# Attention and gated feed-forward on one core: the first third of the instructions of every engine in a listed order, the mask tables in fewer steps, tiles at other addresses

## The chip, the cores and the metric

The kernel runs on one core of a Trainium2 chip, as one launch. The metric is the device time of one execution in microseconds (us), as the median of several. A core has a matrix engine (TensorE, PE in the profile; its weight loads are a row of their own, PEld), a vector engine (VectorE, DVE), an activation engine (ScalarE, ACT), a general engine (GpSimd, POOL) and an engine that issues transfers (SyncE, SP). Each runs its own instructions strictly in the order in which they stand in the program, and semaphores make one engine wait for another. Of the memories, SBUF holds the tiles and PSUM takes what PE writes, in banks of 512 fp32 columns.

## The reference

Attention over 4 batches and 8 heads of 768 positions with 64 features each, with a local and a global mask and a bias that grows with distance; its output, 3,072 rows of 512, goes through a gated feed-forward of width 1,536.

```python
rel = pos[:, None] - pos[None, :]
is_global = pos[None, :] < int(n_global)                # n_global = 8
is_local = (rel >= 0) & (rel < int(n_local))            # n_local = 96
keep = is_global | is_local
dist = np.where(is_global & ~is_local, float(n_local), np.abs(rel))
scores = scale * q @ k.T - slopes * dist
scores = np.where(keep, scores, -1e9)
a = softmax(scores); x = a @ v
gate = 1 / (1 + np.exp(-(x @ w_gate)))
out = (gate * (x @ w_val)) @ w_out
```

The two counts and the three weights are handed over with 64 bits a number; the rest is fp32.

## The kernel before

**Work and tiling.** Rows are taken in 8 blocks of 3 x 128 (two blocks a batch). The attention of a block has four steps `s`, one for each pair of heads. A step has its scores (`scores`, L368 in the first two blocks, L382 later), a minimum with the bias table added (VectorE, L401), the exponential (ScalarE, L414), a transpose (TensorE with `ident`, L447, in the first two blocks; by DMA later), the product with `v` (`values`, L497) and, in the first block, row sums that are spread by a matmul (L523). Every query tile sees 256 keys at most: 96 previous ones, 32 global ones and its own 128. The feed-forward of a block runs over 12 slices `f` of the width: `ff_in` makes gate and value (24 matmuls of 384 columns a slice, L559, into `ps_g` and `ps_u`), `ff_out` adds the slice's part of the output (L599, into three banks `ps_o`).

**Precision by parts.** Most operands are split into a high and a low part (`xh`, `xl`; `w1h`, `w1l`; `w2h`, `w2l`; `hh`, `hl`) and each product is three matmuls. The weights arrive as 64-bit numbers and are turned to fp32 during the first block: `conv_a` and `conv_b` put the bits together on ScalarE and VectorE (L193, L200, L209), `conv_c` splits into `w1h` (ScalarE, L230) and `w1l` (GpSimd, L181, in 8 slices). The second weight is split again for each slice and block (`w2h` on ScalarE, L212; `w2l` on GpSimd, L181).

**Staging.** The attention of the first block stands alone at the start. After it, the attention of block `b + 1` is laid between the feed-forward slices of block `b`. The first block's slices meet their weights as these are converted.

**The start.** Two broadcasts bring the counts (`words`, L77, SyncE). Four VectorE instructions (L81 to L84) make floats of them, and `build_tables` (L107 to L145) makes the distance tables `dist` and `dist0` from counting patterns that GpSimd writes; `build_pair` (L158) scales them into the tables of each head. `keep_busy` (L97) gives TensorE matmuls on zeros, of which nothing is read.

**What sets the order.** The code is written in loops, and the framework's scheduler, which works with a simulated time, decides the order on each engine; `issue_after` holds single instructions behind others. Which addresses a tile has follows from the sizes of the pools that are opened before it.

Of the kernel before, what the change touches and what calls it, by code (L numbers as in the profile page):

```python
# [16 lines left out]
ALU = mybir.AluOpType  # L17
# [3 lines left out]
P = 128  # L21
PREV = 96
GLOB = 32
SLOT = GLOB + P
WIN = PREV + SLOT
NEG = 1.0e30


@with_exitstack
def attn_moe_kernel(ctx, tc, qT, kT, v, n_global, n_local, wg, wv, wo, out, B, H, S, D):  # L30
    nc = tc.nc
    DM = H * D
    NC = DM // P
# [23 lines left out]
    spool = inner.enter_context(tc.tile_pool(name="spool", bufs=2))  # L57
# [2 lines left out]
    wraw = cstack.enter_context(tc.tile_pool(name="wraw", bufs=1))  # L60
    late = {}

    def issue_after(later, earlier):
        tc.add_manual_dep(
            later.ins,
            earlier.ins.name,
            mybir.DependencyInfo(mybir.DependencyClass.NoSync, mybir.DependencyReason.DATA),
            reason="issue order",
        )


    nf = cpool.tile([P, 2], F32, name="nf")


    words = cpool.tile([P, 2, 2], I32, name="words")
    for k, src in enumerate((n_local, n_global)):
        nc.sync.dma_start(  # L77
            words[:, k], src.bitcast(I32)[0:2].rearrange("(a b) -> a b", a=1).to_broadcast([P, 2])
        )
    wf = cpool.tile([P, 3, 2], F32, name="wf")  # L80
    nc.vector.tensor_copy(wf[:, 0:2].rearrange("p w k -> p k w"), words)  # L81
    nc.vector.tensor_scalar(wf[:, 2], wf[:, 0], 0.0, None, op0=ALU.is_lt)
    nc.vector.tensor_tensor(wf[:, 2], wf[:, 2], wf[:, 1], op=ALU.add)
    nc.vector.scalar_tensor_tensor(nf, wf[:, 2], 2.0 ** 32, wf[:, 0], op0=ALU.mult, op1=ALU.add)  # L84
    ident = cpool.tile([P, P], F32, name="ident")
    warm = cpool.tile([P, 1], F32, name="warm")
    nc.vector.memset(warm, 0.0)
# [18 lines left out]
    tabs = [cpool.tile([P, WIN], BF16, name=f"tab{h}") for h in range(H)]  # L106
    tabs0 = [cpool.tile([P, P], BF16, name=f"tabs{h}") for h in range(H)]  # L107
    nms = cpool.tile([P, 2 * (B * NTB * NPAIR)], F32, name="nms")
    def build_tables():

        nl, ng = nf[:, 0:1], nf[:, 1:2]
        reli = spool.tile([P, WIN], I32, name="pT", tag="pT", bufs=PTB)
        nc.gpsimd.iota(reli[:, 0:PREV], pattern=[[-1, PREV]], base=PREV, channel_multiplier=1)
        nc.gpsimd.iota(reli[:, PREV:PREV + GLOB], pattern=[[1, GLOB]], base=0, channel_multiplier=0)
        nc.gpsimd.iota(reli[:, PREV + GLOB:WIN], pattern=[[-1, P]], base=0, channel_multiplier=1)
        coli = mpool.tile([P, P], I32, name="work", tag="work", bufs=WORKB)
        nc.gpsimd.iota(coli, pattern=[[1, P]], base=0, channel_multiplier=0)
        rel = spool.tile([P, WIN], F32, name="pT", tag="pT", bufs=PTB)
        nc.vector.tensor_copy(rel, reli)
        col = mpool.tile([P, 2, P], F32, name="work", tag="work", bufs=WORKB)  # L120
        nc.vector.tensor_copy(col[:, 0], coli)
        loc = spool.tile([P, WIN], F32, name="pT", tag="pT", bufs=PTB)
        pen = mpool.tile([P, 2, P], F32, name="work", tag="work", bufs=WORKB)
        cur = slice(PREV + GLOB, WIN)
        kg, only, both = col[:, 0], col[:, 1], pen[:, 0]
        nc.vector.tensor_scalar(loc, rel, 0.0, None, op0=ALU.is_ge)
        nc.vector.tensor_scalar(kg, kg, ng, None, op0=ALU.is_lt)
        nc.vector.scalar_tensor_tensor(loc, rel, nl, loc, op0=ALU.is_lt, op1=ALU.mult)
        nc.vector.tensor_tensor(rel, rel, loc, op=ALU.mult)
# [3 lines left out]
        nc.vector.tensor_tensor(only, kg, loc[:, cur], op=ALU.is_gt)  # L133
        nc.vector.tensor_tensor(both, kg, loc[:, cur], op=ALU.max)
        nc.vector.scalar_tensor_tensor(only, only, nl, rel[:, cur], op0=ALU.mult, op1=ALU.add)
        nc.vector.tensor_scalar(both, both, 1.0, NEG, op0=ALU.subtract, op1=ALU.mult)
        nc.vector.tensor_tensor(dist0, both, only, op=ALU.subtract)
        build_pair(0, True, (dist, dist0))

        gsl = slice(PREV, PREV + GLOB)  # L140
        nc.vector.tensor_copy(loc[:, gsl], kg[:, 0:GLOB])
        nc.vector.tensor_scalar(rel[:, gsl], kg[:, 0:GLOB], nl, None, op0=ALU.mult)
        nc.vector.tensor_scalar(loc, loc, 1.0, NEG, op0=ALU.subtract, op1=ALU.mult)
        nc.vector.tensor_tensor(dist, loc, rel, op=ALU.subtract)
        return dist, dist0  # L145

    built = set()
    last_min = []
# [3 lines left out]
    def build_pair(s, zero, dist):  # L152
        if (s, zero) in built:
            return
        built.add((s, zero))
        for h in (2 * s, 2 * s + 1):
            eng = nc.gpsimd if s else nc.vector
            eng.tensor_scalar((tabs0 if zero else tabs)[h], dist[zero], slopes[h] / SCALE, None, op0=ALU.mult)  # L158


    w1h = [wpool.tile([P, 2, NC, P], F32R, name=f"w1h{f}") for f in range(NF)]
# [192 lines left out]
    def scores(bi, s, t):  # L354
# [542 lines left out]
```

## Time and profile before

| what | value |
|---|---|
| time, median of 3 runs | 735.9 us (735.83 to 737.05) |
| profiled execution | 739.84 us, of which the instructions span 738.1 us |
| PE busy | 722.8 us, 98% of the span |
| weight loads, DVE, ACT, POOL busy | 655.9, 474.7, 410.8, 228.2 us |
| mean granted TensorE clock | 0.991 |

The profile is one execution, read by a hardware profiler. A busy share is an average over stages, and the ends of matmuls are modelled, so that PE is shown busy where a matmul is only stretched; the distance from one start to the next tells more. Idle time of an engine is printed with what ended it. Times on the line of an instruction are us from the start of the span.

### The profile page before, as it was taken

To read this page: it belongs to the slowest core of one execution; us is meant where nothing else is said; L and a number is where in the kernel's file an instruction comes from. 1 tells how busy PE (TensorE), PEld (TensorE's weight loads), DVE (VectorE), ACT (ScalarE), POOL (GpSimd) and SP (SyncE) were. 2 spreads that over 40 slices of the span, in tenths; PEclk is the share of its full clock that TensorE was granted. 3 is DMA by queue.
4 is the path that set the end of the run, shared out by engine and by line. 5 is a ranking of instruction groups with operands and counts; after the bars stand their busy time and mean duration, and the time that the engine had idled before them with its cause. 6 is when DMAs were issued, how large, how long until landed. Compare 5 with 4: busy or idle time off the path is not lost. (4 is left out here: it accounts for less than half of the span.)

```text
span 738.1 us, 12514 instructions
## 1 busy us (share of the span) xinstructions
PE 722.8 (98%) x4403; PEld 655.9 (89%) x4403; DVE 474.7 (64%) x1279; ACT 410.8 (56%) x938; POOL 228.2 (31%) x238
## 2 busy tenths in 40 slices
PE   8999999999999999999999999999999999999996
PEld 5758788989889999999999999999999999999995
DVE  6765577577877877776777777666787867321111
ACT  4787686656555555565456655555555664332222
POOL 5437366323222323232232323213232231221222
PEclk8999999999999999999999999999999999999999
DMA  8688573524455342442435442353435234010001
GB/s 256 182 256 273 175 211 101 134 56 88 101 89 152 83 110 68 91 113 58 87 84 112 118 102 69 52 133 75 96 78 112 72 44 86 16 44 1 1 0 46
DMA packets 136868, 74.28 MB, mean 101 GB/s; under 512 B 87136, under 2 KB 129120, under 8 KB 136800
## 3 DMA queue, kind: packets, MB, share of 16 engines
q1 hardware_dynamic: 136656, 73.17, 40.0%
q8 instruction: 36, 0.59, 0.4%
q14 instruction: 32, 0.26, 0.1%
q10 hardware_dynamic: 144, 0.26, 0.1%
HBM read 49.81 MB, written 6.29 MB: 76 GB/s over the span
## 5 line engine op out<-in xcount | busy, mean ns | idle before, releaser
L181 POOL TENSOR_TENSOR w2l<-w2f,w2h 128x512 fp32r<-128x512 f32 x89 | 120.3, 1351 | 361.9 <-ACT w2h L212 354.8
L559 PE MATMUL ps_g<-xh,w1l 128*128 128x384 f32 x384 | 132.1, 344 | 1.1 <-ACT work L567 1.1
L559 PE MATMUL ps_u<-xh,w1l 128*128 128x384 f32 x384 | 130.8, 341 | 0.1
L559 PE MATMUL ps_g<-xl,w1h 128*128 128x384 f32 x384 | 129.6, 338 | 0.2 <-DVE xl L540 0.2
L559 PE MATMUL ps_g<-xh,w1h 128*128 128x384 f32 x384 | 129.6, 337 | 0.0
L559 PE MATMUL ps_u<-xl,w1h 128*128 128x384 f32 x384 | 129.3, 337 | 0.0
L559 PE MATMUL ps_u<-xh,w1h 128*128 128x384 f32 x384 | 129.1, 336 | 0.0
L576 DVE SCALAR_TENSOR_TENSOR work<-work,ps_u 128x384 f32<-128x384 f32 x90 | 49.7, 552 | 123.4 <-PE ps_u L559 122.6
L579 ACT ACTIVATE hh<-work 128x384 fp32r<-128x384 f32 x90 | 46.9, 521 | 128.4 <-DVE work L576 128.3
L414 ACT ACTIVATE work<-work,nms 128x256 f32<-128x256 f32 (+1 forms) x192 | 92.0, 480 | 30.0 <-DVE nms L401 29.5
L599 PE MATMUL ps_o<-w2l,hh 128*128 128x512 f32 x267 | 104.7, 392 | 1.8 <-POOL w2l L181 1.8
L599 PE MATMUL ps_o<-w2h,hh 128*128 128x512 f32 x267 | 104.1, 390 | 0.0
L599 PE MATMUL ps_o<-w2h,hl 128*128 128x512 f32 x267 | 103.6, 389 | 0.0
L181 DVE TENSOR_TENSOR hl<-work,hh 128x384 fp32r<-128x384 f32 x90 | 78.8, 875 | 25.4 <-ACT hh L579 25.3
L212 ACT ACTIVATE w2h<-w2f 128x512 fp32r<-128x512 f32 x89 | 56.0, 630 | 55.1 <-PE ps_o L599 54.3
L559 PEld LDWEIGHTS ps_g<-xh,w1l 128*128 128x128 f32 x384 | 72.3, 188 | 5.3 <-issue 2.1
L559 PEld LDWEIGHTS ps_u<-xh,w1l 128*128 128x128 f32 x384 | 72.1, 188 | 4.0 <-issue 1.0
L559 PEld LDWEIGHTS ps_g<-xl,w1h 128*128 128x128 f32 x384 | 72.2, 188 | 2.8 <-issue 1.0
L559 PEld LDWEIGHTS ps_u<-xl,w1h 128*128 128x128 f32 x384 | 72.2, 188 | 1.0
L559 PEld LDWEIGHTS ps_g<-xh,w1h 128*128 128x128 f32 x384 | 72.2, 188 | 0.6 <-issue 0.3
L462 DVE COPY halves<-work 128x512 int16<-128x512 int16 (+1 forms) x144 | 62.8, 478 | 15.0 <-DMA turned<-halves 13.4
L559 PEld LDWEIGHTS ps_u<-xh,w1h 128*128 128x128 f32 x384 | 72.2, 188 | 0.0
(131 smaller groups left out, 1160.6 us busy)
## 6 DMA issues: line engine op xcount, KB each, us to landing
qr<-in_qT SPq DMA_DIRECT2D x56, 192.0 KB, 3.4
kr<-in_kT SPq DMA_DIRECT2D x32, 192.0 KB, 2.7
v<-in_v SPq DMA_DIRECT2D x32, 192.0 KB, 3.4
raw<-in_w_gate SPq DMA_DIRECT2D x12, 512.0 KB, 5.2
raw<-in_w_val SPq DMA_DIRECT2D x12, 512.0 KB, 6.1
raw<-in_w_out SPq DMA_DIRECT2D x12, 512.0 KB, 3.8
out<-ost SPq DMA_DIRECT2D x23, 256.0 KB, 2.1
v<-in_v SPq DMA_DIRECT2D x16, 144.0 KB, 3.7
```

The source lines that it names most:

```text
L181: eng.tensor_tensor(out, a, b, op=ALU.subtract)
L212: ins = nc.scalar.activation(hi, w, AF.Copy)
L414: ins = nc.scalar.activation(sb[:, j, :w], sb[:, j, :w], AF.Exp, scale=-1.0, bias=nm[:, j:j + 1], accum_out=sm[:, j:j + 1])
L462: nc.vector.tensor_copy(dst, words[:, :, :, h])
L559: nc.tensor.matmul(ps[:, :n], wt[f][:, i, c], xt[:, c, :n], start=(k == 0), stop=(k == 3 * NC - 1))
L576: nc.vector.scalar_tensor_tensor(a[:, :n], a[:, :n], 1.0, pss[1][:, :n], op0=ALU.add, op1=ALU.mult)
L579: nc.scalar.activation(hh[:, :n], a[:, :n], AF.Copy)
L599: ins = nc.tensor.matmul(outs[bi][t], ht[:, t * P:(t + 1) * P], wt, start=(f == 0 and k == 0), stop=(f == NF - 1 and k == len(parts) - 1),)
```

## The change

Four things are changed together. **The order:** a table gives, for each engine, the place of each of its first instructions (1,031 on TensorE, 328 on VectorE, 250 on ScalarE, 141 on GpSimd, 141 on SyncE); `arrange` links them in that order, and all others come after the last of them. `issue_after` holds only for those. The number of TensorE, VectorE and ScalarE instructions of the block loops is the same. **The counts:** one broadcast on ScalarE's queue in place of two on SyncE's. **The tables:** seven instructions on VectorE from the landing of the counts to `dist0` in place of nineteen (four of which belong to the last test); the conversion of the counts that only the last test needs (`nf`) stands at the end of the kernel. **The addresses:** tiles of the counts leave a pool and one of 24 bytes becomes 120; `xh` and `xl`, the matrix engine's moving operand of L559, start at a multiple of 128 bytes (32 bytes past one before), `ident` at a multiple of 64, and the tiles `work`, `hh`, `hl`, `w2h`, `w2l`, `kr`, `v0`, `v1` at multiples of 128 (64 past one before).

```diff
+ORDER = dict(
+    tensor=(
+        "0-9 14-16 11 10 13 12 21 20 27 18 17 19 22 53 33 32 26 23-24 28 25 29-31 52 58-59 46-49 36-44 50 45 51 34 54-56 "
...
     def issue_after(later, earlier):
-        tc.add_manual_dep(
...
+        wished.append((later.ins, earlier.ins))
+    def counted(ins):
+        return type(ins).__name__.startswith("Inst") and type(ins).__name__ != "InstRegisterMove"
+    def arrange():
...
+        for name, text in ORDER.items():
+            mine = [i for i in nc.cur_bb.bb.instructions if i.engine == engines[name].engine and counted(i)]
+            order = []
+            for run in text.split():
+                first, _, last = run.partition("-")
+                order += mine[int(first):int(last or first) + 1]
+            for before, ins in zip(order, order[1:]):
+                after(ins, before)
+            placed.update(i.name for i in order)
+            for ins in mine:
+                if ins.name not in placed:
+                    after(ins, order[-1])
+        for later, earlier in wished:
+            if later.name not in placed:
+                after(later, earlier)
...
-    for k, src in enumerate((n_local, n_global)):
-        nc.sync.dma_start(
-            words[:, k], src.bitcast(I32)[0:2].rearrange("(a b) -> a b", a=1).to_broadcast([P, 2])
-        )
-    nc.vector.tensor_copy(wf[:, 0:2].rearrange("p w k -> p k w"), words)
-    nc.vector.tensor_scalar(wf[:, 2], wf[:, 0], 0.0, None, op0=ALU.is_lt)
-    nc.vector.tensor_tensor(wf[:, 2], wf[:, 2], wf[:, 1], op=ALU.add)
-    nc.vector.scalar_tensor_tensor(nf, wf[:, 2], 2.0 ** 32, wf[:, 0], op0=ALU.mult, op1=ALU.add)
+    nc.scalar.dma_start(words.rearrange("p k w -> p (k w)"), counts.bitcast(I32).rearrange("(a b) -> a b", a=1).to_broadcast([P, 4]))
+    low = cpool.tile([P, 2], F32, name="low")
...
+        nc.vector.tensor_scalar(off, reli, 0.0, NEG, op0=ALU.is_lt, op1=ALU.mult)
+        nc.vector.tensor_tensor(rel, reli, off, op=ALU.max)
+        nc.vector.tensor_copy(low, words[:, :, 0])
...
+        nc.vector.tensor_scalar(off, rel, nl, NEG, op0=ALU.is_ge, op1=ALU.mult)
+        nc.vector.tensor_scalar(dist0, col, ng, NEG, op0=ALU.is_ge, op1=ALU.mult)
+        nc.vector.tensor_tensor(dist, rel, off, op=ALU.max)
+        nc.vector.tensor_scalar(dist0, dist0, nl, None, op0=ALU.max)
+        nc.vector.tensor_copy(dist[:, gsl], dist0[:, 0:GLOB])
+        nc.vector.tensor_tensor(dist0, dist0, dist[:, cur], op=ALU.min)
...
+    arrange()
     inner.close()
...
-    last = small.tile([P, 6], F32, name="top", bufs=1)
+    nf = gpool.tile([P, 2], F32, name="nf")
...
+    last = small.tile([P, 30], F32, name="top", bufs=1)[:, 0:6]
```

The rows that follow give line numbers of the changed file, which are higher than those of the kernel before: L182 is `keep_busy` (L97 before), L442 the scores (L368), L521 the transposes (L447), L475 the minimum (L401), L232 the scaled tables (L158), L255 the subtraction that makes the low parts (L181).

First TensorE, from its first instruction on. Before:

```order
L97 MATMUL ps_v<-zeros 128x128 x10
L368 MATMUL ps_g<-kr,qr_176 128x128
L368 MATMUL ps_s<-kr,qr_176 128x128
L368 MATMUL ps_o_239<-kr,qr_176 128x256
L368 MATMUL ps_u<-kr,qr_176 128x256
L97 MATMUL ps_v<-zeros 128x128 x4
L368 MATMUL ps_g<-kr,qr_176 128x256
L368 MATMUL ps_s<-kr,qr_176 128x256
L447 MATMUL ps_t<-ident,work 128x128 x2
```

And with the change:

```order
L182 MATMUL ps_v<-zeros 128x128 x13
L442 MATMUL ps_s<-kr,qr_170 128x128
L442 MATMUL ps_g<-kr,qr_170 128x128
L442 MATMUL ps_u<-kr,qr_170 128x256
L442 MATMUL ps_o_224<-kr,qr_170 128x256
L442 MATMUL ps_s<-kr,qr_170 128x256
L442 MATMUL ps_g<-kr,qr_170 128x256
L442 MATMUL ps_u<-kr,qr_180 128x128
L521 MATMUL ps_t<-ident,work 128x128
L182 MATMUL ps_v<-zeros 128x128
```

Thirteen of the fourteen matmuls on zeros now stand ahead of the first scores, and the scores of the first step follow one another.

Second VectorE, between the patterns that GpSimd writes (`pT`, `work`) and the first minimum. Before:

```order
L81 CAST wf<-words 128x2x2
L82 TENSOR_SCALAR wf<-wf 128x2
L83 TENSOR_TENSOR wf<-wf 128x2
L84 SCALAR_TENSOR_TENSOR nf<-wf 128x2
L127 TENSOR_SCALAR work<-work,nf 128x128
L128 SCALAR_TENSOR_TENSOR pT<-pT,nf 128x256
L766 TENSOR_SCALAR top<-nf 1x1 x4
L129 TENSOR_TENSOR pT<-pT 128x256
L133 TENSOR_TENSOR work<-work,pT 128x128
```

And with the change:

```order
L209 CAST low<-words 128x2
L213 TENSOR_SCALAR dist_204<-work,low 128x128
L212 TENSOR_SCALAR work<-work,low 128x256
L215 TENSOR_SCALAR dist_204<-dist_204,low 128x128
L214 TENSOR_TENSOR dist<-work 128x256
L216 COPY dist<-dist_204 128x32
L217 TENSOR_TENSOR dist_204<-dist_204,dist 128x128
L232 TENSOR_SCALAR tab_115<-dist 128x256
L232 TENSOR_SCALAR tabs_123<-dist_204 128x128
L475 ISA work,nms<-ps_s,tabs_123 128x128
```

Nine instructions now lie between the counts' landing and the first minimum (`ISA`); before, twelve more than are shown lay there.

Third GpSimd, where the first low part of the second weight is made (`w2l`; the slices `w1l` are those of later `f`). Before:

```order
L181 TENSOR_TENSOR w1l_157<-bits,w1h_145 128x128 x8
L181 TENSOR_TENSOR w2l<-w2f_168,w2h 128x512
L181 TENSOR_TENSOR w1l_158<-bits,w1h_146 128x128 x8
L181 TENSOR_TENSOR w2l<-w2f_169,w2h 128x512
L181 TENSOR_TENSOR w1l_159<-bits,w1h_147 128x128 x8
```

And with the change:

```order
L255 TENSOR_TENSOR w1l_152<-bits,w1h_140 128x128
L255 TENSOR_TENSOR w2l<-w2f_162,w2h 128x512
L255 TENSOR_TENSOR w1l_152<-bits,w1h_140 128x128 x2
L255 TENSOR_TENSOR w1l_151<-bits,w1h_139 128x128 x4
L255 TENSOR_TENSOR w1l_152<-bits,w1h_140 128x128 x2
L255 TENSOR_TENSOR w1l_151<-bits,w1h_139 128x128
L255 TENSOR_TENSOR w2l<-w2f_163,w2h 128x512
```

The slices of two values of `f` are mixed, and a `w2l` stands among them instead of behind a full group of eight.

## Rows read from the trace of the kernel before

**Rows 1.** The page, part 1, PE's row: busy time, share, instructions.
```profile
PE   722.8 (98%) x4403; PEld 655.9 (89%) x4403; DVE 474.7 (64%) x1279; ACT 410.8 (56%) x938; POOL 228.2 (31%) x238
```

**Rows 2.** Stretches: length, busy PE, PEld, DVE, ACT, POOL (counts); clock; DMA share, GB/s.
```profile
4.30:11.10 6.80, 4.21 (x34) 2.91 (x33) 6.07 (x35) 1.67 (x7) 2.70 (x5) 1.00 1.02 268
11.10:21.30 10.20, 10.20 (x54) 6.78 (x52) 5.21 (x20) 8.12 (x24) 5.83 (x8) 0.50 0.86 305
...
31.50:43.00 11.50, 9.95 (x90) 7.49 (x89) 7.33 (x17) 7.14 (x15) 5.18 (x10) 1.00 0.78 232
43.00:117.00 74.00, 74.00 (x415) 57.23 (x416) 48.37 (x117) 58.98 (x118) 37.93 (x73) 1.00 0.68 210
117.00:225.00 108.00, 104.19 (x642) 96.00 (x641) 78.49 (x211) 63.26 (x150) 36.95 (x31) 1.00 0.43 95
225.00:727.00 502.00, 502.00 (x3053) 471.84 (x3052) 318.20 (x838) 262.14 (x596) 131.16 (x91) 1.00 0.33 75
```

**Rows 3.** Timeline of the first 10 us, all engines.
```profile
0.85 0.39 SPq L77 DMA_DIRECT2D words<-in_n_local  x1
...
1.03 4.03 PE L97 MATMUL ps_v<-zeros 128*128 128x128 f32 x20 [1.03 <-DVE zeros L91]
...
1.29 0.42 SPq L77 DMA_DIRECT2D words<-in_n_global  x1
...
4.77 0.17 DVE L81 CAST wf<-words 128x4 f32<-128x4 int32 x1 [2.37 <-DMA words<-in_n_global]
...
6.17 0.34 PE L368 MATMUL ps_g<-kr,qr 64*128 64x128 f32 x1 [1.12 <-DMA kr<-in_kT]
...
9.12 0.27 DVE L401 CUSTOM_DVE_ANT_0 work<-ps_s,tabs 128x128 f32<-128x128 f32 x1
...
9.66 0.48 PE L368 MATMUL ps_g<-kr,qr 64*128 64x256 f32 x1 [1.48 <-DVE nms L401]
```

**Rows 4.** DMA issues of the first 8 us: count, size, median us to landing.
```profile
qr<-in_qT SPq DMA_DIRECT2D x2, 192.0 KB, 3.5
...
words<-in_n_local SPq DMA_DIRECT2D x1, 1.0 KB, 2.6
words<-in_n_global SPq DMA_DIRECT2D x1, 1.0 KB, 3.4
```

**Rows 5.** Timeline of PE: one visit to 64-column tiles between two `ff_in` matmuls.
```profile
61.84 0.34 PE L559 MATMUL ps_g<-xh,w1l 128*128 128x384 f32 x1
62.02 0.34 PE L559 MATMUL ps_g<-xl,w1h 128*128 128x384 f32 x1
62.29 1.53 PE L497 MATMUL ps_t<-pT,v 128*64 128x128 f32 x24
63.75 0.44 PE L559 MATMUL ps_g<-xh,w1h 128*128 128x384 f32 x1
64.02 0.34 PE L559 MATMUL ps_u<-xh,w1l 128*128 128x384 f32 x1
```

**Rows 6.** ACT's groups in the first 40 us.
```profile
L414 ACT ACTIVATE work<-work,nms 128x256 f32<-128x256 f32 x16 | 8.0, 501 | 2.2 <-DVE nms L401 2.2
...
L230 ACT ACTIVATE w1h<-bits 128x1024 fp32r<-128x1024 f32 x2 | 2.1, 1058 | 0.4 <-DVE bits L209 0.4
L531 ACT COPY hl<-ps_o 128x384 f32<-128x384 f32 x4 | 1.9, 469 | 2.0 <-PE ps_o L523 2.0
```

**Rows 7.** Timeline of PE: the first matmul of `ff_in`, and the first of slice 1.
```profile
30.69 0.42 PE L559 MATMUL ps_g<-xh,w1l 128*128 128x384 f32 x1
...
42.98 0.42 PE L559 MATMUL ps_g<-xh,w1l 128*128 128x384 f32 x1 [0.58 <-ACT work L567]
```

**Rows 8.** PE's greatest wait over the span: us in total, times, longest.
```profile
PE ps_o L599 <- POOL w2l L181: 1.8, 2, 1.0
```

**Rows 9.** GpSimd's timeline, the groups around that first `w2l`.
```profile
113.16 4.38 POOL L181 TENSOR_TENSOR w1l<-bits,w1h 128x128 fp32r<-128x128 f32 x8 [3.12 <-ACT w1h L230]
...
117.50 1.27 POOL L181 TENSOR_TENSOR w2l<-w2f,w2h 128x512 fp32r<-128x512 f32 x1
```

More of the change, by code (lines that the diff above doesn't have):

```diff
@@ L26, with attn_moe_kernel @@
 NEG = 1.0e30
+ORDER = dict(
+    tensor=(
[25 rows of a table added]
+    ),
+    vector=(
[10 rows of a table added]
+    ),
+    scalar=(
[8 rows of a table added]
+    ),
+    gpsimd=(
[4 rows of a table added]
+    ),
+    sync=(
[4 rows of a table added]
+    ),
+)
 @with_exitstack
-def attn_moe_kernel(ctx, tc, qT, kT, v, n_global, n_local, wg, wv, wo, out, B, H, S, D):
+def attn_moe_kernel(ctx, tc, qT, kT, v, counts, wg, wv, wo, out, B, H, S, D):
     nc = tc.nc
@@ L61, in attn_moe_kernel @@
     late = {}
+    wished = []
     def issue_after(later, earlier):
-        tc.add_manual_dep(
[L65 to L68, printed above, removed]
-        )
-    nf = cpool.tile([P, 2], F32, name="nf")
-    words = cpool.tile([P, 2, 2], I32, name="words")
-    for k, src in enumerate((n_local, n_global)):
-        nc.sync.dma_start(
-            words[:, k], src.bitcast(I32)[0:2].rearrange("(a b) -> a b", a=1).to_broadcast([P, 2])
-        )
@@ L80, in attn_moe_kernel @@
-    wf = cpool.tile([P, 3, 2], F32, name="wf")
-    nc.vector.tensor_copy(wf[:, 0:2].rearrange("p w k -> p k w"), words)
-    nc.vector.tensor_scalar(wf[:, 2], wf[:, 0], 0.0, None, op0=ALU.is_lt)
-    nc.vector.tensor_tensor(wf[:, 2], wf[:, 2], wf[:, 1], op=ALU.add)
-    nc.vector.scalar_tensor_tensor(nf, wf[:, 2], 2.0 ** 32, wf[:, 0], op0=ALU.mult, op1=ALU.add)
+        wished.append((later.ins, earlier.ins))
+    def counted(ins):
+        return type(ins).__name__.startswith("Inst") and type(ins).__name__ != "InstRegisterMove"
@@ new lines, in arrange, with after @@
+    def arrange():
+        engines = dict(tensor=nc.tensor, vector=nc.vector, scalar=nc.scalar, gpsimd=nc.gpsimd, sync=nc.sync)
+        placed = set()
+        def after(later, earlier):
+            tc.add_manual_dep(
+                later,
+                earlier.name,
+                mybir.DependencyInfo(mybir.DependencyClass.NoSync, mybir.DependencyReason.DATA),
+                reason="issue order",
+            )
+        for name, text in ORDER.items():
[13 more added lines that the diff above has]
+                after(later, earlier)
@@ L109, in build_tables @@
     def build_tables():
-        nl, ng = nf[:, 0:1], nf[:, 1:2]
+        nl, ng = low[:, 0:1], low[:, 1:2]
+        cur, gsl = slice(PREV + GLOB, WIN), slice(PREV, PREV + GLOB)
         reli = spool.tile([P, WIN], I32, name="pT", tag="pT", bufs=PTB)
         nc.gpsimd.iota(reli[:, 0:PREV], pattern=[[-1, PREV]], base=PREV, channel_multiplier=1)
-        nc.gpsimd.iota(reli[:, PREV:PREV + GLOB], pattern=[[1, GLOB]], base=0, channel_multiplier=0)
-        nc.gpsimd.iota(reli[:, PREV + GLOB:WIN], pattern=[[-1, P]], base=0, channel_multiplier=1)
@@ L116, in build_tables @@
[L116 to L129, printed above, removed]
+        nc.gpsimd.iota(reli[:, gsl], pattern=[[0, GLOB]], base=-1, channel_multiplier=0)
+        nc.gpsimd.iota(reli[:, cur], pattern=[[-1, P]], base=0, channel_multiplier=1)
@@ L130, in build_tables @@
+        col = mpool.tile([P, P], I32, name="work", tag="work", bufs=WORKB)
+        nc.gpsimd.iota(col, pattern=[[1, P]], base=0, channel_multiplier=0)
+        far = mpool.tile([P, 2, WIN], F32, name="work", tag="work", bufs=WORKB)
+        rel, off = far[:, 0], far[:, 1]
+        nc.vector.tensor_scalar(off, reli, 0.0, NEG, op0=ALU.is_lt, op1=ALU.mult)
+        nc.vector.tensor_tensor(rel, reli, off, op=ALU.max)
+        nc.vector.tensor_copy(low, words[:, :, 0])
         dist = wraw.tile([P, WIN], BF16, name="dist", bufs=1)
@@ L131, in build_tables @@
         dist0 = wraw.tile([P, P], BF16, name="dist0", bufs=1)
[L133 to L137, printed above, removed]
-        build_pair(0, True, (dist, dist0))
-        gsl = slice(PREV, PREV + GLOB)
@@ L141, in build_tables @@
[L141 to L144, printed above, removed]
+        nc.vector.tensor_scalar(off, rel, nl, NEG, op0=ALU.is_ge, op1=ALU.mult)
+        nc.vector.tensor_scalar(dist0, col, ng, NEG, op0=ALU.is_ge, op1=ALU.mult)
+        nc.vector.tensor_tensor(dist, rel, off, op=ALU.max)
@@ L157, in build_pair @@
             eng = nc.gpsimd if s else nc.vector
-            eng.tensor_scalar((tabs0 if zero else tabs)[h], dist[zero], slopes[h] / SCALE, None, op0=ALU.mult)
+            eng.tensor_scalar((tabs0 if zero else tabs)[h], dist[zero], -slopes[h] / SCALE, None, op0=ALU.mult)
     w1h = [wpool.tile([P, 2, NC, P], F32R, name=f"w1h{f}") for f in range(NF)]
@@ L751, in attn_moe_kernel @@
     late["pool"] = gpool
-    last = small.tile([P, 6], F32, name="top", bufs=1)
+    nf = gpool.tile([P, 2], F32, name="nf")
+    wf = gpool.tile([P, 3, 2], F32, name="wf")
+    issue_after(nc.vector.tensor_copy(wf[:, 0:2].rearrange("p w k -> p k w"), words), last_min[-1])
+    nc.vector.tensor_scalar(wf[:, 2], wf[:, 0], 0.0, None, op0=ALU.is_lt)
+    nc.vector.tensor_tensor(wf[:, 2], wf[:, 2], wf[:, 1], op=ALU.add)
+    nc.vector.scalar_tensor_tensor(nf, wf[:, 2], 2.0 ** 32, wf[:, 0], op0=ALU.mult, op1=ALU.add)
+    last = small.tile([P, 30], F32, name="top", bufs=1)[:, 0:6]
     top = last[:, 0:1]
@@ L880 @@
         "v": _np.ascontiguousarray(v.transpose(0, 2, 1, 3)).reshape(B * S, H * D),
-        "n_global": _np.asarray(inputs["n_global"]).reshape(1),
-        "n_local": _np.asarray(inputs["n_local"]).reshape(1),
+        "counts": _np.stack([inputs["n_local"], inputs["n_global"]]),
         "w_gate": _slices(inputs["moe_w_gate"]),
```

50 rows, old and new, of tables (gpsimd, scalar, sync, tensor) are left out of this document.

## The prediction, made before the changed kernel was run

> **What bounds the kernel now.** I read the page first: PE is busy for 722.8 us, 98% of the span [rows 1], so only time that PE loses can be won. Then the stretches [rows 2]: from 225 to 727 us PE has no idle time in 502 us, and from 43 to 117 us none in 74. The losses lie elsewhere. From 4.3 to 11.1 us PE works 4.21 of 6.80 us; from 11.1 to 21.3 it is busy all along, but the granted clock is 0.50; from 31.5 to 43 it is idle for 1.55 us; from 117 to 225 for 3.81. Last I read the timeline of the start [rows 3] and PE's waits [rows 8] to see what these losses wait for.
>
> **Where the change can act.** I compared the two programs instruction by instruction. On TensorE they are the same from the 1,112th instruction on, which is where the 576th matmul of `ff_in` has been issued; the last stretch of [rows 2] begins there. So the sum is the time by which PE reaches that point earlier or later. It is made against the profiled execution, 739.84 us (span 738.1 and 1.7 around it), and is then taken from the median of the runs, 735.9, which lies 3.9 lower.
>
> **Term 1: the first minimum.** Before, the second transfer of the counts is issued at 1.29 us, VectorE takes it up at 4.77, and the first minimum starts at 9.12 [rows 3]. The two transfers landed 2.6 and 3.4 us after their issue [rows 4]. One transfer from ScalarE's free queue can be issued at about 0.85, as SyncE's first was, and lands 2.6 to 3.4 later, at 3.5 to 4.3; I take 3.6, near the one that had no other ahead of it. Then nine instructions on VectorE instead of 24: (9.12 - 4.77) / 24 = 0.18 us each before. The new ones are on average wider, so I take 0.22: 2.0 us, and the table stands at 5.6. PE must be ready too: 20 records of matmuls on zeros, ten instructions, ran from 1.03 to 5.06 [rows 3]; three more instructions end them at about 5.6. The query tile, now SyncE's fifth transfer, is issued at 0.85 + 4 x 0.47 = 2.7 (0.42 of issuing [rows 3] and a little between) and lands 3.5 later [rows 4], at 6.2. Scores took about half a microsecond to be ready, so the first minimum comes between 6.1 (table and zeros) and 6.8 (query tile). I take 6.5: 2.6 us earlier.
>
> **Term 2: the first slice.** The next mark is PE's first matmul of `ff_in`, 30.69 us before [rows 7]. It needs `w1l`, made on GpSimd from `w1h`, made on ScalarE. In the new order ScalarE does, before `w1h`, 18 exponentials (0.50 us each at most: 9.0), the two bit conversions of 1,024 columns, which I price like `w1h` (1.06 each: 2.1), and six short copies (0.47: 2.8) [rows 6]: 13.9 us, and 1.06 for `w1h`. From a first exponential at 6.8 that ends at 21.8. Six of the exponentials have 128 columns and are shorter, which would give 20 to 21; against that stand waits, since ScalarE was idle for 10.2 - 8.12 = 2.1 us in the stretch at half clock [rows 2]. I take 22. GpSimd then needs about 3 us for the five slices that PE wants first and for `xh` and `xl` between them (4.38 / 8 = 0.55 a slice [rows 9]). First matmul at 25.0, bounds 23.5 to 27.5: 5.7 us earlier. PE's own work does not forbid it: before, it stood at 30.69 with 10.2 us at half clock [rows 2] and 1.12 and 1.48 us of idle time [rows 3] behind it; without these 5.1 + 2.6 us it would have stood near 23.
>
> **Term 3: from there to slice 1.** Before, 12.3 us lie between the two rows of [rows 7], for 24 matmuls of 0.17 to 0.18 us (4.2 [rows 5]), the rest of the first block's attention, and 1.55 us of idle time. In the new order one step's `values` less is left (about 1.5 us [rows 5]), and fewer visits to other tile shapes; I take 10 us and half of the idle time, so slice 1 starts at 35.0 against 42.98: **8.0 us earlier**. Its weights must be there: by ScalarE's sum, 22 + 9.2 us of further work plus 0.5 for a slice, 31.7, with 3 us to spare.
>
> **Term 4: keeping it.** From 43 to 117 us ScalarE is busy for 59.0 of 74 us, VectorE 48.4, GpSimd 37.9, and the DMA engines for 0.68 [rows 2]. All have at least a fifth to spare, so conversion can run 8 us ahead of where it stood, and PE keeps the lead. Cost: nothing, so long as no listed place makes PE wait.
>
> **Term 5: waits from 117 to 225 us.** PE loses 3.81 us [rows 2], 1.8 of it to `w2l` [rows 8]. The longer of these two waits, at 117.5 us, comes from the order itself: GpSimd does eight slices for 4.38 us first and then the `w2l` of 1.27 for which PE waits [rows 9]. The new order mixes them and divides `ff_out` among other matmuls. I take half: -1.9. Bounds: 0 and -3.8.
>
> **Term 6: tile shapes.** A matmul followed by one of its own shape starts 0.18 us before the next (61.84 to 62.02); before a matmul on 64 columns it is 0.27, and the first one after it takes 0.27 instead of 0.17 [rows 5]. With what the visit itself loses, a change of shape costs PE 0.1 to 0.2 us. By three shapes I count 68 changes among the first 1,031 instructions before and 49 now (the change's own count is 56). Nineteen at 0.1 to 0.2 are 1.9 to 3.8 us, but sixteen of them lie in the first 200 instructions, which terms 1 to 3 already cover. Left: three, **-0.5**.
>
> **Term 7: new waits.** The list is one fixed order of five engines over 215 us, and any place where a transfer or a partner is later than it assumes stops an engine and all behind it. The old order had 3.8 us of such waits in 108 us and none in 74. I take **+2.0**, bounds 0 and 6.
>
> **Term 8: addresses.** No row of before shows an address's price, since each tile had one address. `ff_in` reads `xh`, which moves, and its starts are 0.17 to 0.18 apart [rows 5], so an effect over 5% is not excluded by anything; I take 0 and bound it by 1 ns of these for each of 2,304 matmuls: 2.3 us either way.
>
> Sum: -8.0 - 1.9 - 0.5 + 2.0 = **-8.4 us**: 731.4 for a profiled execution and **727.5** for the median.
>
> **The clock.** The granted clock fell at 11.1 us, after 1.12 and 1.48 us of idle time shortly after each other [rows 3], and stayed at half, 1.2 instead of 2.4 GHz, for 10.2 us [rows 2]. With the first minimum at 6.5 both gaps shrink to under a microsecond. I take it that the fall is gone in most executions; if it is not, PE needs about 5 us more for the work of that stretch, of which about 2 lie beside ScalarE's sum (23 + 5 against 25 to 26). The Trainium skill speaks against counting on it: "TensorE: Matmul & The Clock Gate", section "What's actually happening", says that the monitor of activity runs on its own time and does not start with the kernel, so that the same kernel can meet it at different points. By that rule some executions would show the half clock and some not; the trace of one execution can't show it.
>
> **Rivals.**
> - *Everything is won* (0.17): no new waits, the whole of term 5, and perhaps something from the addresses. 8.0 + 3.8 + 0.5 = 12.3, with 2.3 more from addresses 14.6: 721.3 to 723.6. For it: idle time and half clock together lose more than this before. Against it: every order so far leaves some waits.
> - *Half is given back* (0.18): new waits at their bound of 6 or the half clock again with a late `w1l` (27.5): 730.5 to 734.4. For it: the list mixes single slices of two `f` on GpSimd, where a late one holds PE.
> - *It does nothing* (0.05): what is won before 43 us is waited away because conversion can't follow. 735.9. Against it: the spare fifth on each engine [rows 2].
> - *Slower* (0.08): the `w2l` of slices 6 to 11 stand behind single slices of `w1l`; if ScalarE's `w2h` comes late, GpSimd stops, the `w1l` behind it too, and PE waits twice a slice. The price is up to 1.3 us [rows 9] at each of 12 places (six in each of the first two blocks), 15.6 in all; it decides from 0.9 us a place on, since 10.4 us is what terms 1 to 6 win and 10.4 / 12 = 0.87. Then 738 to 741. Against it: the wait of 1.0 [rows 8] came after a block of 4.38 us, which no longer stands there.
> - *My forecast* (0.52): 724.5 to 730.5.
>
> **How the numbers follow.** The likeliest gives 727.5. The range leaves out about one in ten on each side: low 721.3, the best case with addresses; high 734.3, the end of the half-given-back case. A difference under 0.2% (1.5 us) is about what a measurement of this kernel can't tell from none: 734.4 to 737.4. Faster: 0.52 + 0.17 + 0.18 = 0.87; same 0.05; slower 0.08.
>
> **What would show it.** Term 1: the first L401 row (L475 in the new file) near 6.5 us, the counts taken up before 4.3. Term 2 and 3: the first `ff_in` matmul near 25 us and slice 1 near 35. The clock: no stretch at 0.50 between 6 and 25 us. Term 5 and 7: PE's idle time from slice 1 on under 4 us in all. Term 8: the stretch of 502 us, the same instructions in both, longer or shorter. I'd be wrong if ScalarE or DVE hold the first block, so that `ff_in` starts after 27.5, or if new waits on w2l, hh or ps_o appear between 40 and 215 us; or if addresses change every matmul by more than a nanosecond.

## The result, and the profile after

The changed kernel takes **743.2 us** (742.4 to 743.9), the kernel before 735.9 (735.3 to 737.1): 1.0093 of its time, 95% interval 1.0076 to 1.011. The forecast was 727.5 with a range up to 734.3, so the kernel became slower where it was forecast to become faster. The profiled execution took 743.79 us and spans 742.0.

Of 35 executions of the kernel before that were timed beside the first four experiments, 25 with a mean granted clock of 0.998 or more took 734.6 to 736.7 us and ten with 0.991 or 0.992 took 738.4 to 740.4, and the profile shown ahead of the prediction, with the half clock from 11.1 to 21.3 us [rows 2], is of the second kind while the median is of the first.

The stretches of the changed kernel, with the borders of [rows 2]:

```profile
4.30:11.10 6.80, 5.52 (x40) 4.52 (x39) 3.58 (x22) 3.06 (x14) 5.51 (x9) 1.00 0.86 273
11.10:21.30 10.20, 9.64 (x105) 7.57 (x103) 8.86 (x36) 8.94 (x32) 4.38 (x7) 1.00 0.92 256
...
31.50:43.00 11.50, 10.61 (x55) 8.00 (x55) 8.57 (x23) 9.04 (x20) 5.74 (x13) 1.00 0.55 199
43.00:117.00 74.00, 73.98 (x411) 57.11 (x411) 45.41 (x106) 57.16 (x113) 40.32 (x79) 1.00 0.64 211
117.00:225.00 108.00, 104.87 (x629) 94.60 (x628) 70.65 (x212) 61.60 (x146) 30.93 (x22) 0.98 0.48 102
225.00:727.00 502.00, 501.19 (x3025) 470.04 (x3024) 316.19 (x833) 260.32 (x593) 128.90 (x90) 1.00 0.33 73
```

The start works as meant: full clock from 4.3 to 117 us, 105 matmuls in the second stretch instead of 54. The last stretch is as full as before, but in its 502 us PE starts 3,025 matmuls and not 3,053 [rows 2], though both programs issue the same matmuls there. The marks of the prediction, from the timelines of VectorE and PE:

```profile
5.28 0.19 DVE L232 TENSOR_SCALAR tabs<-dist 128x128 bf16<-128x128 bf16 x1
7.62 0.29 DVE L475 CUSTOM_DVE_ANT_0 work<-ps_s,tabs 128x128 f32<-128x128 f32 x1 [2.15 <-PE ps_g L442]
...
7.13 0.34 PE L442 MATMUL ps_s<-kr,qr 64*128 64x128 f32 x1 [1.21 <-DMA qr<-in_qT]
...
26.28 0.42 PE L633 MATMUL ps_u<-xh,w1l 128*128 128x384 f32 x1
...
35.88 0.34 PE L633 MATMUL ps_g<-xh,w1l 128*128 128x384 f32 x1
...
224.40 0.34 PE L633 MATMUL ps_g<-xh,w1l 128*128 128x384 f32 x1
```

The first row of `ff_in` comes at 26.28 us instead of 30.69 and slice 1 at 35.88 instead of 42.98 [rows 7]. The last row shown is the 577th matmul of `ff_in`, where slice 24 begins and from where on the two programs are the same on PE; before, it stood at 227.7. So 7.1 us were won by slice 1 and 3.3 were left at slice 24; the last matmul ends at 734.1 us and not 732.2, and the span at 742.0 and not 738.1. The end itself, on VectorE:

```profile
734.17 0.42 DVE L691 TENSOR_SCALAR ost<-ps_o 128x256 f32<-128x256 f32 x1
737.33 0.17 DVE L828 CAST wf<-words 128x4 f32<-128x4 int32 x1 [2.74 <-DMA out<-ost]
...
738.13 0.32 DVE L846 TENSOR_SCALAR top<-nf 1x1 f32<-1x1 f32 x4
738.49 0.15 DVE L848 TENSOR_REDUCE flag<-top 1x1 int32<-1x5 f32 x1
740.00 0.06 DVE L926 MEMSET top<- 1x1 f32 x1 [1.37 <-issue]
```

The conversion of the counts, moved to the end, waits 2.74 us for an output transfer: its tiles `nf` and `wf` lie in memory that the output tile `ost` held (e5 and e6 below bear this out). PE's waits between slice 1 and slice 24, and the place of the longest:

```profile
PE ps_u L633 <- DVE work L650: 2.9, 2, 1.5
PE ps_o L673 <- ACT hh L653: 0.2, 1, 0.2
```
```profile
184.56 0.44 PE L633 MATMUL ps_u<-xh,w1l 128*128 128x384 f32 x1 [1.47 <-DVE work L650]
```

The two waits for `w2l` of [rows 8] are gone; two others for `work` have come. Around the longer one the clock falls (PE's columns first: busy, weight loads; then VectorE, ScalarE, GpSimd, the clock):

```profile
184.00:185.50 1.50, 0.73 (x2) 0.48 (x3) 1.50 (x7) 0.96 (x4) 0.00 (x0) 1.00 0.22 41
185.50:189.00 3.50, 3.50 (x13) 3.19 (x12) 1.44 (x6) 2.14 (x6) 0.67 (x1) 0.51 0.43 76
189.00:192.00 3.00, 3.00 (x16) 2.74 (x16) 1.74 (x3) 1.37 (x3) 1.17 (x1) 1.00 0.68 175
```

PE idles for 1.47 us up to 184.56, of which the first row holds half, then 3.5 us pass at half clock, which cost about (1 - 0.51) x 3.5 = 1.7. The same wait stands in e1, e5 and e6 below (1.2 to 1.3 us) with no fall of the clock behind it.

### The profile page after: what moved, and what is told of

Read it like the earlier page. It is cut to its first block, busy times and chain, and to the rows that moved or that the text cites. A ratio compares the mean times of both kernels' runs of the same rounds, so it can differ in the third digit from the quotient of the medians.

```text
span 742.0 us, 12497 instructions
## 1 busy us (share of the span) xinstructions
PE 725.9 (98%) x4403; PEld 658.9 (89%) x4403; DVE 465.9 (63%) x1273; ACT 412.2 (56%) x938; POOL 225.4 (30%) x238
## 4 chain that ended last, share of the span: by engine, by line
PE 90%; DMA 4%; DVE 3%; SPq 1%; issue 1%; ACT 1%; POOL 0%; DVEq 0%; ACTq 0%
PE ps_o L673 27%; PE ps_g L633 26%; PE ps_u L633 26%; PE ps_s L456 4%; PE ps_t L571 3%; DMA turned<-halves 2%; DMA kr<-in_kT 2%; PE ps_v L571 2%; PE ps_t L521 1%; DVE work L507 1%; PE ps_s L442 1%; PE ps_v L442 1%; DVE halves L536 0%; DVE ks L255 0%; SPq L370 0%
## 5 line engine op out<-in xcount | busy, mean ns | idle before, releaser
L255 POOL TENSOR_TENSOR w2l<-w2f,w2h 128x512 fp32r<-128x512 f32 x89 | 119.7, 1345 | 366.2 <-ACT w2h L286 363.3
L633 PE MATMUL ps_u<-xh,w1l 128*128 128x384 f32 x384 | 134.3, 350 | 2.9 <-DVE work L650 2.9
L633 PE MATMUL ps_u<-xh,w1h 128*128 128x384 f32 x384 | 130.6, 340 | 0.0
L673 PE MATMUL ps_o<-w2l,hh 128*128 128x512 f32 x267 | 106.2, 400 | 0.3 <-ACT hh L653 0.2
L255 DVE TENSOR_TENSOR hl<-work,hh 128x384 fp32r<-128x384 f32 x90 | 74.8, 831 | 27.6 <-ACT hh L653 27.6
L641 ACT ACTIVATE work<-ps_g 128x384 f32<-128x384 f32 x96 | 46.6, 485 | 46.4 <-PE ps_g L633 45.0
```

Of the source, the lines that this page charges most:

```text
L255: eng.tensor_tensor(out, a, b, op=ALU.subtract)
L633: nc.tensor.matmul(ps[:, :n], wt[f][:, i, c], xt[:, c, :n], start=(k == 0), stop=(k == 3 * NC - 1))
L641: last_gate[:] = [nc.scalar.activation(a[:, :n], ps[:, :n], AF.Tanh, scale=0.5)]
L673: ins = nc.tensor.matmul(outs[bi][t], ht[:, t * P:(t + 1) * P], wt, start=(f == 0 and k == 0), stop=(f == NF - 1 and k == len(parts) - 1),)
```

## The experiments

**My theory** after these rows: the places of the tiles in SBUF make PE's matmuls slower, the end loses 2 us by its wait, and the listed order wins less than forecast. **The rival:** the order itself, by what it makes run side by side, slows the matmuls. For each kernel two spacings tell a matmul's time: the mean distance from one start to the next where two matmuls of 384 columns (`ff_in`) or of 512 columns (`ff_out`) follow each other, worked out from the trace's start times from 3 us behind the start of slice 24 to 715 us (about 1,550 and 550 pairs). The kernel before has 174.86 and 227.62 ns, the changed one **176.62 and 229.34**. All but e1, e5, e6 and e9 are the kernel before with tiles moved.

### Undoing the addresses, and doing them alone

e1 is the changed kernel at the old addresses:

```diff
-    low = cpool.tile([P, 2], F32, name="low")
+    low = cpool.tile([P, 16], F32, name="low")[:, 0:2]
-    last = small.tile([P, 30], F32, name="top", bufs=1)[:, 0:6]
+    last = small.tile([P, 6], F32, name="top", bufs=1)
```

> The changed kernel with everything kept (the list, the counts, the pools at 128 bytes, the conversion of the counts at the end); only two small tiles are padded so that xh, xl, work, hh, hl, w2h, w2l and the rest start at the addresses of the kernel before. If addresses make the matmuls slower: the matmul of L633 comes back from about 175.5 to 173.5 ns and that of L673 from 229.8 to 228, the stretch from slice 24 to the last slice from 498.9 to about 493.7 us, and the time from 743.2 to about 736.7 us (735.5 to 738.5). If the listed order made them slower, or the chip of that run did: 743.2 us again, matmuls as in the changed kernel.

Measured: 738.0 us, 1.0022 of before (0.9999 to 1.0046); 174.85 and 227.57 ns; from slice 24 to the end of the last matmul 505.2 us instead of 509.7. That is what the theory gave.

e2 is the kernel before at the new addresses:

```diff
-    nf = cpool.tile([P, 2], F32, name="nf")
+    wf = cpool.tile([P, 4, 2], F32, name="wf")
+    nf = wf[:, 3]
...
-    wf = cpool.tile([P, 3, 2], F32, name="wf")
...
-    last = small.tile([P, 6], F32, name="top", bufs=1)
+    last = small.tile([P, 30], F32, name="top", bufs=1)[:, 0:6]
```

> The kernel before in its own order; only two tiles are merged and one padded, so that all tiles start at the addresses of the changed kernel. If addresses make the matmuls slower: 742.4 us (741 to 743.5), 6.5 us above the kernel before, with its L559 spacing 1.5 to 2 ns longer. If the listed order is the cause: 735.9 us, nothing moves.

Measured: 740.4 us, 1.0055 (1.003 to 1.008); 176.62 and 229.41 ns. The time is below the 741 to 743.5 that the theory gave: the addresses alone cost 0.55%, 4.0 us, and not 6.5. The spacings go with the addresses, to less than 0.1 ns, in either order of instructions: the rival has fallen. The stretch from 228 to 720 us, columns as in [rows 2], of the changed kernel and then of e1:

```profile
228.00:720.00 492.00, 491.19 (x2971) 460.57 (x2970) 314.70 (x831) 258.16 (x589) 126.09 (x87) 1.00 0.33 74
```
```profile
228.00:720.00 492.00, 492.00 (x2998) 462.52 (x2997) 312.78 (x821) 258.17 (x588) 129.53 (x89) 1.00 0.32 74
```

PE is full in both but for 0.8 us, and 27 more matmuls fit at the old addresses.

### Which tiles

e3 does the first half of the move (the diff of e2 with 14 in place of 30), e4 the second (only the last line, with 22). e16 is e3 with an 8-column tile put ahead of the small statistics tiles, and 6 for 14, so that these stay. e15 puts a 16-column tile ahead of `w2h`.

```diff
+    small.tile([P, 8], F32, name="pad", bufs=1)      (e16)
+    w2pool.tile([P, 16], F32, name="pad")            (e15)
```

> The kernel before with only the 32-byte move: xh and xl (and ident) 32 bytes lower, on a multiple of 128 bytes, all later tiles where they were. If the address of the moving operand xh and xl is what counts: L559 longer by 1.5 to 2 ns, L599 unchanged, about 4.5 us above the kernel before (740.4). If it is the later tiles (hh, hl, w2h, w2l, work): 735.9 us.

> The kernel before with only the 64-byte move: work, hh, hl, w2h, w2l, kr, v and all later tiles 64 bytes higher, on a multiple of 128 bytes; xh and xl where they were. If xh and xl carry the cost: L559 unchanged, L599 longer by 1.5 to 2 ns, about 1.5 us above the kernel before (737.4). If the later tiles carry all of it, through writes that meet the matmul's reads: about 742 us.

> As e3, xh and xl 32 bytes lower (and the constants ahead of them), but the small statistics tiles stay too. If the place of xh and xl is what made L559 slower in e3: L559 about 177 ns, 739 to 741 us. If L599's 1.7 ns there came from the small tiles: L599 227.6 ns; if also from xh and xl: 229.4 ns. If the small tiles carried all of it: 174.9 and 227.6 ns and 736 us.

> The kernel before with only w2h, w2l and the tiles behind them (kr, v and on) 64 bytes higher; work, hh, hl, xh and xl stay. If the place of w2h and w2l is what made L599 slower in e4: L599 about 230.8 ns as there, L559 about 174.8, 738 us. If it was work, hh and hl: L599 227.6 ns and 736 us.

| kernel | moved, in bytes | 384 columns, ns | 512 columns, ns | ratio to before (95%) |
|---|---|---|---|---|
| e3 | `xh`, `xl`, small: -32 | 176.98 | 229.36 | 1.0061 (1.0042 to 1.008) |
| e16 | `xh`, `xl`: -32 | 176.98 | 229.36 | 1.0089 (1.0066 to 1.0113) |
| e4 | `work`, `hh`, `hl`, `w2h` and on: +64 | 174.71 | 230.82 | 1.003 (1.0008 to 1.0052) |
| e15 | `w2h`, `w2l` and on: +64 | 175.05 | 230.44 | 1.0036 (1.0016 to 1.0056) |

e16 and e15 answer as their first conditions put it (e16, of four executions only, 0.4 us above its 741): each moving operand's place slows its own matmul, `xh` and `xl` that of `ff_in` by 2.1 ns, `w2h` and `w2l`, with the tiles behind them, that of `ff_out` by about 3, where e4 was expected to give 1.5 to 2. The move of `xh` and `xl` also costs `ff_out` 1.7 ns, which I had not expected, and the two moves together (e2) cost less than their sum.

### Which place is a good one

The change put both on multiples of 128 bytes, so the next question was whether the multiple itself is the cost.

```diff
+    wf = cpool.tile([P, 16], F32, name="wf")[:, 0:6]...   (e7; e12: 24; e10: 40)
+    last = small.tile([P, 30], F32, ...)[:, 0:6]          (e7; e12: 24; e8: 14; e11: 40)
```

> The kernel before with xh and xl 32 bytes higher (64 past a multiple of 128 bytes, where e3 put them on the multiple), the later tiles 128 bytes higher, so that their place within 128 bytes is as before. If only a start on a multiple of 128 bytes costs: 736 us, L559 spacing 174.9 ns in the stretch after slice 24. If any start other than 32 past a multiple of 64 costs: L559 near 177 ns, 741 us as e3.

> The kernel before with work, hh, hl, w2h, w2l and all later tiles 32 bytes higher (96 past a multiple of 128 bytes; before 64 past it, in e4 on it), xh and xl where they were. If w2h and w2l cost only on a multiple of 128: L599 spacing 227.6 ns as before and 736 us. If what counts is where they stand to xh and xl: L599 between 228 and 231 ns, up to 2 us more. If 32 bytes past a multiple of 64 is the best place for them as it is for xh: L599 below 227.6 ns and up to 1 us less than before.

> The kernel before with xh, xl, small, work, hh, hl, w2h, w2l and all later tiles 128 bytes higher; the loaded weights w1h, w1l and w2f stay. If only the place within 128 bytes counts, for each tile or between tiles: spacings 174.9 and 227.6 ns and 736 us, as the kernel before. If a move by any amount against the tiles that stay costs: 738 to 741 us.

> The kernel before with work, hh, hl, w2h, w2l and all later tiles 128 bytes higher, xh and xl where they were. If only the place within 128 bytes counts: 174.9 and 227.6 ns, 736 us. If it slows L559 too, whose own operands stand still here, then the clash is between the matmul's reads and what the other engines read and write, and it goes by more than 128 bytes: L559 176 ns, 738 to 740 us.

> The kernel before with xh and xl 64 bytes higher (96 past a multiple of 128 bytes) and the later tiles 128 bytes higher (the place within 128 bytes as before). If 32 past a multiple of 64 is the good place for xh and xl: L559 174.9 ns and 736 us. If the one arrangement of before is the good one among these, whatever the alignment: L559 between 175.4 and 177 ns and 738 to 741 us.

| kernel | `xh`, `xl` | `work` to `w2l` and on | 384, ns | 512, ns | ratio (95%) |
|---|---|---|---|---|---|
| e7 | +32 | +128 | 175.39 | 229.90 | 1.0045 (1.0023 to 1.0067) |
| e8 | 0 | +32 | 176.26 | 229.20 | 1.0055 (1.0038 to 1.0073) |
| e10 | +128 | +128 | 176.64 | 229.98 | 1.0047 (1.0024 to 1.0069) |
| e11 | 0 | +128 | 175.89 | 231.08 | 1.0054 (1.0032 to 1.0076) |
| e12 | +64 | +128 | 174.62 | 230.60 | 1.0011 (0.9992 to 1.003) |

Where the expectations named 736 us for a place within 128 bytes they missed, all but nearly e12, whose `ff_in` is as quick as before and whose `ff_out` is not. No alignment explains this: e10 and e11 keep every tile's place within 128 bytes and are as slow as the rest. In e8 and e11 even `ff_in` is slower, although nothing that it reads has moved: between 400 and 700 us its spacing in e8 is 176.8 ns where GpSimd alone works beside PE and 174.9 where no engine does, against 173.4 and 173.6 in the kernel before. What these moves have in common is that tiles move against the loaded weights (`w1h`, `w1l`, `w2f`), which stayed. So e13 and e14 move everything:

```diff
     wpool = ctx.enter_context(tc.tile_pool(name="wpool", bufs=1))
+    wpool.tile([P, 32], F32, name="pad")                  (e13; e14: 16)
```

> The kernel before with every tile 128 bytes higher, the loaded weights w1h, w1l and w2f too, so that no tile moves against another. If what counts is where the tiles stand to each other: spacings 174.9 and 227.6 ns as in the kernel before and 736 us. If the absolute place counts, by more than the last 128 bytes: 175.5 to 177 and 229 to 231 ns, 738 to 742 us, as in e10.

> As e13, with every tile 64 bytes higher. Tiles against each other: 174.9 and 227.6 ns, 736 us. Absolute place: 175.5 to 177 and 229 to 231 ns, 738 to 742 us.

Measured: e13 736.2 us, 1.0003 (0.9979 to 1.0026), 174.86 and 227.62 ns; e14 735.6 us, 1.0007 (0.9986 to 1.0028), 174.86 and 227.61. The spacings are those of the kernel before to 0.01 ns. **What counts, for steps of 64 and 128 bytes, is where the tiles stand to one another, not where they stand.** The same stretch for PE alone (busy time, count, clock, DMA), of e10 and then of e13:

```profile
228.00:720.00 492.00, 492.00 (x2976) 1.00 0.34 74
```
```profile
228.00:720.00 492.00, 492.00 (x3000) 1.00 0.34 75
```

### The end, and the list

e6 is e1 with the conversion's tiles beside the counts, e5 the changed kernel with them in the pool of small tiles (and 14 for 30 in the last line, so that no address moves), e9 is e6 with the loop over the list left out, so that `issue_after` sets the order as before.

```diff
-    nf = gpool.tile([P, 2], F32, name="nf")
-    wf = gpool.tile([P, 3, 2], F32, name="wf")
+    nf = low16[:, 2:4]                                    (e6, e9; low16 holds low too)
+    wf = low16[:, 4:10].rearrange("p (w k) -> p w k", w=3)
...
-        for name, text in ORDER.items():
+        for name, text in ():                             (e9)
```

> As e1 (the changed kernel at the addresses of the kernel before), but the tiles that the counts are converted into no longer lie over the output tile whose last transfer is still running: they lie beside the counts, so the conversion after the last minimum has nothing to wait for. If that wait is the whole price of moving the conversion: the time from the last matmul of the attention and feed-forward part to the end of the span falls from 7.9 us in e1 to 6, and the median from 738.0 to about 736.0 us, level with the kernel before. If the four operations of the conversion themselves are the price, or the last transfer ends the span anyway: 738.0, as e1.

> The changed kernel at its own addresses, with the one part undone that e6 undid: the converted counts in a tile of their own instead of over the output tile. If list, addresses and end simply add: the time after the last matmul 5.3 us instead of 7.9, the matmul spacings as in the changed kernel (176.6 and 229.3 ns), and about 741 us (740 to 742). If the changed kernel's end is set by the last output transfer instead: 743.2.

> As e6, but without the listed order: the counts in one transfer and the new tables alone, the instructions ordered by the same hand-written rules as in the kernel before. If the list carries the earlier start: first matmul of slice 1 near 39 us as in e2 and e4 (43 where the clock falls), and the time that of the kernel before, 736 us. If counts and tables carry it: slice 1 near 36 us, and about 2 us less than the kernel before.

Measured: e6 736.5 us, 0.9993 (0.9971 to 1.0014); e5 741.9, 1.0049 (1.0028 to 1.0069); e9 737.7, 1.0003 (0.9987 to 1.0019). The end of e6:

```profile
727.10 0.39 PE L674 MATMUL ps_o<-work,hl 128*128 128x512 f32 x1
...
729.04 0.06 DVE L927 MEMSET top<- 1x1 f32 x1 [1.09 <-issue]
```

PE's last matmul ends at 727.5 and the span at 732.8, 5.3 us later, against 742.0 - 734.1 = 7.9 in the changed kernel and also in e1. By the ratios the wait is worth 0.3% (e1 to e6, whose intervals overlap) to 0.4% (changed kernel to e5, whose intervals do not), 2 to 3 us. e9's profile has a granted clock of 0.54 from 18.3 to 25.7 us, so its mark of slice 1, at 41.5 us, is no clean one; its median, at before's level within 0.2%, tells that the counts and tables alone win nothing that can be measured. Nor does the list: e6 and e9, timed beside each other, differ by it alone, and their ratios by 0.1%, less than either interval.

## Why the prediction was wrong, step by step

e14 has the kernel before's order and spacings, and its profile fell on an execution at full clock, so it stands in for the kernel that the median measures. Its marks:

```profile
39.36 0.41 PE L560 MATMUL ps_g<-xh,w1l 128*128 128x384 f32 x1 [0.56 <-ACT work L568]
...
223.26 0.34 PE L560 MATMUL ps_g<-xh,w1l 128*128 128x384 f32 x1
...
727.32 0.39 PE L600 MATMUL ps_o<-work,hl 128*128 128x512 f32 x1
```

and those of e1, the list at the same relative places:

```profile
35.71 0.34 PE L633 MATMUL ps_g<-xh,w1l 128*128 128x384 f32 x1
...
220.90 0.34 PE L633 MATMUL ps_g<-xh,w1l 128*128 128x384 f32 x1
...
725.74 0.39 PE L673 MATMUL ps_o<-work,hl 128*128 128x512 f32 x1
```

| mark, us | e14 | e1 | changed | e1 - e14 | changed - e14 |
|---|---|---|---|---|---|
| slice 1 | 39.4 | 35.7 | 35.9 | -3.7 | -3.5 |
| slice 24 | 223.3 | 220.9 | 224.4 | -2.4 | +1.1 |
| last matmul ends | 727.7 | 726.1 | 734.1 | -1.6 | +6.4 |
| span | 733.5 | 734.0 | 742.0 | +0.5 | +8.5 |

So the 8.5 us of these profiled executions are: the list's -1.6 at the last matmul; addresses and the half clock at 185.5 us, 734.1 - 726.1 = +8.0, of which 1.7 is the clock and 6.3 is left for addresses and scatter; and the end, +2.1. The medians differ by 7.3.

Ahead of slice 24 single profiles scatter: e6, with e1's order and addresses, ends its last matmul at 727.5 and not 726.1, so the list's share is -0.2 to -1.6. Behind slice 24 they repeat. To the end of the last matmul it takes 504.4 us in the kernel before, e9, e13 and e14, and 508.7 at the new addresses in e2 (its marks follow) and e5, so addresses cost 4.3 there. The changed kernel's 509.7 and e1's 505.2 hold besides a wait of PE just behind slice 24, shown for the changed kernel and then for e1:

```profile
224.78 0.34 PE L559 MATMUL ps_g<-xh,w1l 128*128 128x384 f32 x1
...
733.11 0.39 PE L599 MATMUL ps_o<-work,hl 128*128 128x512 f32 x1
```
```profile
PE ps_s L456 <- DVE nms L475: 0.8, 1, 0.8
```
```profile
PE ps_s L456 <- DVE nms L475: 0.5, 1, 0.5
```

The forecast of 727.5 is missed by 15.7 us, and two failures of about equal size make that up. The list, which was to win 8.4 us, wins next to nothing: without addresses and end (e6) the time is 0.9993 of before where the forecast is 0.9886, 8 us apart. The addresses and the end, which were to cost nothing, cost 4 to 5.5 and 2 to 3 us, and these turned the sign.

- **Term 8 (addresses: 0, bounded by 2.3 us) is the step that failed and made the kernel slower.** The bound of 1 ns for 2,304 matmuls was too small in both factors: the runs show 1.76 ns on these (4.1 us) and 1.72 ns on the 846 of `ff_out` (1.5 us), which the term left out: 5.5 together. The measured ratios give 1.0093 - 1.0022, 0.7% or 5.2 us, between the changed kernel and e1, and 0.55% or 4.0 us for the addresses alone (e2). The bound had no row behind it; "an effect over 5% is not excluded" was the honest bound, and 1 ns a choice within it.
- **The end had no term at all.** The move of `nf`'s conversion was listed among the changes and cost 2 to 3 us (e5, e6): the four operations had stood at the start, and at the end they wait for a transfer on the path that sets the time.
- **Term 1 (first minimum at 6.5) was off by its query tile.** The tables were ready at 5.47, as worked out (5.6), but the scores waited for `qr`, which was there at 7.13 and not 6.2; the first minimum came at 7.62.
- **Terms 2 and 3 (slice 1 at 35.0, 8.0 earlier) had the mechanism right and the saving wrong, which is the largest part of the win that did not come.** The marks came at 26.28 and 35.88, against 25.0 and 35.0. But they were taken from an execution with the half clock, and the 3.9 us between it and the median were subtracted as if the saving were the same in both. In the executions that make the median that clock is full, and slice 1 was never at 43.0: of the profiles of the old order, the eight with full clock in the first 45 us have it at 39.2 to 40.1 us, the five with the half clock at 43.0 to 43.6. The lead is 3.7 us (e1) to 4.0 (e6, at 35.3) and not 8.
- **Term 4 (keeping it: 0), terms 5 and 6 (-1.9, -0.5) and term 7 (+2.0).** From slice 1 to slice 24 e1 gives back 1.3 us and e6 2.9. PE's idle time there is 2.1 us in e1 and 3.9 in e6, against 3.2 in e14: waits changed their place more than their sum. The rest of that stretch takes 2.2 to 2.3 us more. By the three tile shapes that term 6 counted, the changes there are 29 against 32, few as it said; but where a change of columns counts too, PE goes from one form of matmul to another 247 times against 114, and term 6 left that out. That these changes are the cause was not tried apart. Behind slice 24 the wait for `nms` takes another 0.8 (e1) to 0.9 (e6), so that of the lead -1.6 to -0.2 us reach the last matmul.
- **The clock.** The fall at 11.1 us did not return in the profiles of the list (the changed kernel, e1, e5, e6), as expected, and of their forty timed executions two have a mean clock under 0.994, against ten of the 35 before. But one fall came at 185.5 us in the changed kernel. The rule cited from the Trainium skill, "TensorE: Matmul & The Clock Gate", section "What's actually happening", agrees with the timed runs: of e2's twelve, four had a mean clock of 0.991 to 0.993 and 743.9 to 744.8 us, eight 0.998 or more and 739.2 to 741.0.
- **The rival "slower"** (738 to 741) put its price on `w2l` in the first blocks; no such wait came. It was right in sign alone, by another cause.

No kernel here beats the kernel before: the list at the old addresses without the wait (e6) is level with it.

## What to carry to other kernels

When a change shifts tiles, even small ones ahead of the operands of the main loop, hold the addresses fixed first (a padded tile or two does it, as in e1) and measure the move as a change of its own: 1.7 to 1.8 ns on each of 3,150 matmuls outweighed all that the order won. Make the sum against an execution of the same kind as those that the median is of; a stall that only some executions have is not won in the others. And an operation moved to the end is priced by what it waits for there, its memory included, and not by its length.

## What the runs showed of the hardware

The spacing of matmuls depends on where the tiles stand to one another in SBUF. The ten arrangements tried in which tiles move against one another gave 174.6 to 177.0 ns for 384 columns and 229.2 to 231.1 for 512, before 174.86 and 227.62; moving all tiles together by 64 or 128 bytes changed neither by more than 0.01 ns. None of the ten was faster in sum. The effect is no scatter: in the profiles of the kernel before, e9, e13 and e14 the 3,058 matmuls from slice 24 on start at the same distances to within 7 ns over 504 us, and e3 and e16, which differ by the place of the small tiles alone, to within 1 ns. The Trainium skill, "SBUF — State Buffer", section "Who interferes with whom", states that only the port pair that GpSimd and VectorE share causes contention. By that rule no other engine's work could slow PE, wherever the tiles stand. e16 and e15 measured that the place of an operand does change PE's spacing, and where the two differ, the measurement decides. Whether other engines' accesses, transfers or PE's own reads of weights and operands meet there, no run tells apart. The traces give hints only. Taken between 400 and 700 us, with an engine counted as beside PE when it is busy at any moment between two starts, e16's move makes `ff_in` slower even where no other engine is at work (176.1 ns against 173.6). Its `ff_out` is hardly slower there (227.4 against 227.0) but is beside VectorE alone (230.3 against 228.6) and ScalarE alone (228.1 against 226.9), while with e15's move `ff_out` is slower where none is at work too (229.9 against 227.0). Open too is the spread of the listed order: e1's twelve runs lie between 735.8 and 741.6 us, more than the clock of each explains.
